# Another stated order for the 2997 steps of a one-core delta-rule and MLP kernel on Trainium2

## The chip, the cores and the metric

The kernel runs on one core of a Trainium2 chip. The metric is the device time of one execution in microseconds (us). A core has five engines that matter here: PE (TensorE, matrix products), DVE (VectorE), ACT (ScalarE), POOL (GpSimd) and SP (SyncE, which here only issues DMAs). Each engine runs its own instructions in order; they wait for each other by semaphores.

## The reference

First a linear attention with a delta rule, step by step over the sequence, for 4 batches x 8 heads, 768 positions, head dimension 48, in fp32; then a layer norm and an MLP with a residual:

```python
k_n = k / (np.linalg.norm(k, axis=-1, keepdims=True) + 1e-06)
for t in range(S):
    y[:, :, t] = einsum('bhd,bhde->bhe', q[:, :, t], state)
    v_old = einsum('bhde,bhd->bhe', state, k_n[:, :, t])
    state = state + beta[:, :, t] * einsum('bhd,bhe->bhde', k_n[:, :, t], v[:, :, t] - v_old)
# x = y with its heads side by side: (4, 768, 384)
xn = (x - mean(x)) / sqrt(var(x) + 1e-06) * g_ln
out = x + maximum(xn @ w_ch1, 0.0) @ w_ch2     # 384 -> 1536 -> 384
```

## The kernel before, in words

The sequence is cut into 12 chunks of 64 positions. Inside a chunk the recurrence becomes matrix products: the products of the keys with themselves (L775), the inverse of a triangular 64 x 64 matrix for each of the 32 heads, the products of queries and keys (L775), and then what goes from chunk to chunk: keys and queries with the state (L983), u (L1017), y (L1024) and the update of the state (L1034).

The inverses are made in three ways. For chunk 0 `first_inverse` works in five levels, for two groups g0 and g1 of 16 heads each: a product E (L722), predicated copies into the matrix on DVE (L731), a product Z (L741), transposes on DVE (L687) and copies back on ACT (L681). For the later chunks `rows_inverse` makes the inverses of 32 x 32 blocks of two chunks in 31 rounds of two DVE instructions (L860, L867); the matrices come in by a DMA (gb) and the inverse goes through DRAM (xd) back to xt. `join` puts two blocks of 32 together: a transposition on DVE (L888) and products e (L898) and z (L904).

After each chunk 256 rows of the MLP are done: layer norm on ACT and DVE (rstd at L967), transposes on PE (L1096) and copies to xnt on ACT (L1088), then the two products with the weights. For the first chunk the first product goes by halves of the columns (L1326, L1341). Later both use fast matrix multiplication: seven products in place of eight for the second (`seven`: products L1423, combinations on POOL L1410, sums on DVE L1441), fifteen in place of sixteen for part of the first (`fifteen`, L1221), and plain products (L1300) for the rest.

No scheduler orders the work when it is built. The functions above only add steps to a list, `Line`; a step is one engine's work (one instruction, or for PE a group of products, most often 16 to 64 small ones or one to four large ones) and it knows which steps it depends on. The text ORDER, at the head of the file, names all 2997 steps in one sequence; `a:b` stands for a run of numbers, and `z` for a filler, two products by the unit matrix whose result is not used (L1515). The steps are emitted in that sequence, and `in_this_order` ties each instruction to the one before it on its own engine and each DMA outside POOL's queue to the one before it in the other queue, so what stands in ORDER is each engine's own order.

```python
def stated_order():
    for t in ORDER.split():
        a, _, b = t.partition(":")
        yield from (-1,) if a == "z" else range(int(a), int(b or a) + 1)
...
for n in stated_order():
    if n < 0:
        self.filler()
        continue
    fn, deps = self.steps[n]
    assert deps <= out and n not in out
    fn()
    out.add(n)
```

Steps named by number in what follows: the inverse of chunk 0 has E and Z of level 1 at 122, 124 and 126, 132 (g0, g1), level 2 at 138, 141 and 144, 150, level 3 at 156, 159 and 162, 168, level 4 at 174, 177 and 180, 186, level 5 at 192, 194 and 196, 200; 175 and 176 are predicated copies of level 4, 193 is the one of level 5 and g0, 187 and 188 are transposes of level 4 and g1. 204 and 205 are the products of queries and keys of chunk 0. 355 and 357 are its u, 359 and 360 its y, 361 to 364 layer norm, 373 to 376 the transposes to xnt, 379 the update of the state. 590 and 588 are the first steps of the first MLP. 337 copies turned keys of chunk 2 on ACT, 389 converts weights there, and 339 and 351 are the products of the keys (L775) of chunks 2 and 3. 327 to 330 read back what the first `rows_inverse` left in xd. 480 to 487 load gb for the second, 556 is the last of its rounds, 557 writes xd and 558 to 565 read it. 625, 699, 704, 961, 967 and 968 are other DMAs that SP issues. 2947 to 2954, 2965 to 2967 belong to the last `seven`: 2953 and 2954 are combinations on POOL.

Of the kernel before, what the change touches and what calls it, by code (L numbers as in the profile page):

```python
# [59 lines left out]
1 9 49 50 8 63 52 51 10 5 250 54 71 11 56 0 6 14 7 12 47 62 53 48 23 13 72 55 36 18 64 42 26 37 61 27 58 60 77 81 15 28 17 32 331 43 73 88 29 40 65 79  # L60
24 19 82 68 78 21 89 74 95 16 76 20 90 75 98 83 80 84 22 85 34 91 86 96 87 33 25 92 97 93 4 35 30 94 110 99 100 111 101 112 114 66 116 122 113 211 210
117 102 70 208 123 115 103 118 233 126 104 124 69 127 105 107 128 119 31 121 106 125 120 252 129 223 132 38 221 138 108 134 39 139 109 222 251 140 135
204 131 130 234 136 3 674 144 137 67 57 133 213 254 146 224 141 149 2 209 413 235 44 142 147 45 253 244 212 143 256 145 150 255 242 205 41 154 153 416
155 243 148 238 151 236 332 152 225 675 156 z 215 157 240 159 158 214 237 239 160 216 162 161 257 46 241 168 164 166 333 206 165 334 245 207 417 163
419 169 174 170 343 258 226 175 172 259 173 415 171 176 381 177 425 260 227 261 167 178 344 217 228 180 179 248 414 263 345 335 386 346 219 182 262
677 186 264 181 420 183 265 266 192 267 268 189 246 336 269 270 218 193 229 220 188 185 184 187 59 271 196 422 190 272 191 231 273 426 194 274 197 199
275 198 421 338 276 247 355 382 277 195 249 384 356 337 359 278 678 279 679 280 200 230 281 361 232 363 387 339 282 364 201 383 391 283 202 203 385
389 373 357 284 375 388 376 374 396 285 590 390 340 358 341 588 591 286 681 342 401 379 287 392 288 289 594 394 290 953 291 347 589 595 292 348 380
293 360 393 350 598 294 362 395 592 368 599 349 442 295 680 441 406 296 351 427 369 815 593 444 297 814 428 443 298 676 602 424 299 352 687 596 300
603 353 301 445 302 399 303 304 377 597 612 305 817 306 606 354 307 418 308 613 607 309 365 423 600 310 397 311 614 689 312 601 366 313 610 314 816  # L70
315 615 611 316 409 604 317 819 318 319 616 818 605 320 404 321 617 322:324 407 608 398 483 325 378 400 402 326 367 629 487 609 370 481 403 371 618
630 480 429 372 446 627 486 485 619 682 628 405 482 633 484 631 329 634 408 330 447 632 410 327 328 448 449 956 479 821 635 820 411 637 809 620 810
638 488 636 621 489:491 641 492 494 622 639 430 493 691 623 495 640 690 496 642 431 497 686 498 624 499 500 822 643 435 434 693 645 501 433 962 502
688 432 503 644 651 957 1100 504 505 436 692 506 507 652 438 508 439 509 647 440 510 437 811 653 511 512 964 450 666 1102 513 654 514 1099 451 515 655
516 517 454 518 965 519 966 1104 520 656 961 455 521 951 456 452 522 463 958 457 646 458 657 453 1215 464 649 465 807 523 459 658 808 524 466 460 1105
525 659 963 467 461 1106 694 950 468 683 462 955 526 660 1112 527 684 1101 528 469 1111 529 473 648 650 695 530 475 474 531 470 476 532 471 661 472
696 533 857 534 1114 535 697 536 967 855 537 858 1213 538 539 685 662 540 856 541 823 542:545 825 546:548 861 663 549:551 863 552 862 553:556 667 867
557 864 968 668 665 869 824 879 868 702 880 959 664 960 859 1214 669 873 860 560 1272 559 672 1103 865 561 812 670 558 705 826 477 866 699 874 698 870
701 888 969 412 706 871 703 885 700 875 704 671 872 1216 566 881 889 625 876 877 895 563 1217 813 567 878 1222 890 564 569 915 882 570 827 562 891 568
886 898 571 565 916 707 1107 896 626 899 572 1115 1212 900 708 883 576 892 709 574 884 901 573 1224 710 1116 893 575 902 954 887 894 917 903 1380 1113  # L80
828 904 1221 1558 711 713 905 829 923 918 577 712 897 924 832 714 715 673 925 716 833 717 906 718 834 926 719 912 835 907 841 836 927 1274 842 919 928
837 1560 908 838 929 920 843 913 839 909 844 941 840 720 910 721 830 845 921 914 846 847 722 922 1377 851 723 578 1264 1223 849 930 724 1557 1226 579
942 725 580 1562 831 931 1218 852 943 850 1118 853 932 848 726 581 1117 933 854 727 582 944 911 728 934 945 729 935 730 970 936 1227 731 938 1376 583
732 937 971 1225 972 585 1273 1228 584 587 1210 1563 733 946 734 1006 952 735 939 736 737 1004 738 974 973 947 1005 739 1007 586 1028 1010 740 1029
1119 1564 1559 975 1229 1011 1031 1008 1561 741 1385 742 1570 940 743 1569 1012 744 1009 745 746 1016 747 1013 976 748 749 1014 1387 750 1017 1572
1386 751 478 1211 979 752 1571 1015 1378 753 754 977 980 755 981 756 1018 1389 757 988 982 989 1384 1573 978 990 1379 1020 983 758:760 1022 761 1021
762 991 984 763 1390 1019 764 1108 985 765 949 1023 1034 1391 766 1230 986 767 948 1109 768 769 1388 1037 770 987 771 1110 1026 772 773 992 774 775
993 994 1038 776 1027 1024 995 1670 1044 1231 996 1030 1120 1265 1025 1275 1047 1035 1121 1039 1064 1040 1048 1122 1045 780 1041 1032 777 1049 1033
778 1065 1042 1036 779 1050 1043 1066 1126 1046 1051 1000 1054 1219 1266 1233 998 1268 997 1232 1276 999 1267 1127 1052 1055 1131 1053 1067 1565 1128
1061 1056 1072 1124 1270 1068 1125 1073 1392 1220 1069 1129 1074 1002 1057 1130 1001 1070 1075 785 1003 784 1058 1269 1076 781 1234 1079 1277 782 1059  # L90
1080 1271 783 1060 1077 1081 1680 2035 1078 786 1373 1062 1090 787 1123 1082 790 1091 789 1083 788 1063 1278 1092 2037 1279 1084 1682 1132 1071 1093
1681 1085 791 1302 1133 1086 1280 793 1134 792 1135 794 1136 1138 795 1094 1284 1137 2039 1139 1140 1235 1141 1285 1142 1281 1143 796 1305 1095 1303
1236 1668 1290 2034 1096 1684 1144 1087 1374 1145 2041 1282 1146 1291 1673 2036 1147 1148 1574 1088 1149 1237 1150 1283 1669 1151 1152 1239 1098 1153
1154 797 1155 1156 1296 1157 799 800 1158 1241 1686 1159 1288 1576 1160 1297 1304 1248 1161 2040 1311 1162 1289 1286 1238 1249 1250 1163 1381 1294
1164 1858 1287 1382 1165 1240 1383 1679 801 1312 1675 1295 1292 1251 1089 1166 1167 1685 1313 1168 1293 1674 1393 1252 1242 1169 798 1253 1855 1308
1243 1395 1375 1309 1244 1857 1306 1245 802 1318 1397 1097 1314 1300 1394 1319 1307 1298 1170 1575 1301 1171 803 805 1172 1246 1321 1173 1315 1247
1174 1322 1299 1255 1316 804 1310 806 1323 1254 1317 1396 1175 1256 1320 1683 1176 2038 1398 1672 1177 1178 1324 1179 1399 1338 1180 1325 1676 1181
1339 1326 1340 1327 1328 1182 1341 1260 1346 1183 1342 1184 1257 1347 1185 1343 1186 1259 1348 1344 1329 1687 1258 1349 1335 1353 1330 1350 1187 1354
1863 1188 1331 1189 1853 1351 1190 1402 1336 1191 1263 1345 1352 1261 1400 1262 1192 1404 1193 1194 1355 1865 1411 1195 1332 1412 1196 1356 1197 1413
1364 1198 1333 1414 1365 1334 1337 1450 1199 1441 1366 1200 1401 1440 1451 1455 1201 1427 1403 2150 1577 1357 1405 1430 1406 1367 1851 1358 1457 1439  # L100
1566 1852 1415 1431 1456 1359 1416 1429 1407 1688 1443 1408 1859 1567 1432 1409 1418 1368 1444 1202 1452 1410 1435 1203 1369 1433 1204 1454 1458 1370
1205 2047 1453 1417 1208 1460 1434 1459 1419 1361 1862 1464 1442 1461 1568 1436 1462 1866 1466 1437 1671 1467 1463 1867 1438 1578 1465 1360 1445 1690
1362 1446 1469 1468 1579 1447 1689 1422 1428 1471 1448 1470 1449 1474 2049 1472 1477 1581 1584 1475 1473 1580 1480 1860 1423 1861 1478 1363 1483 1479
1481 1583 1476 1691 1421 1484 2051 1489 1420 1694 1486 1485 1582 1693 1490 1692 1487 1502 1496 1588 1491 1503 1587 1488 1677 1492 1678 1504 1695 1585
1493 1206 1505 1494 1586 1506 1497 1495 1371 1701 1426 1516 1869 1589 1498 1696 1703 1868 1507 1499 1699 1529 1207 1424 2042 1509 1697 1517 1372 1744
# [1547 lines left out]
```

## Time and profile before

| what | value |
|---|---|
| time, median of three runs | 509.16 us (507.25 to 509.48) |
| span of the profiled execution | 508.8 us, 22190 instructions |
| own time of the profiled execution | not given apart from its span |
| PE busy | 488.6 us (96%), 9606 instructions |
| DVE busy | 353.8 us (70%) |
| POOL busy | 275.6 us (54%) |
| ACT busy | 249.0 us (49%) |
| mean granted clock of PE | 0.965 |
| DMA | 54.99 MB, 108 GB/s over the span |

The span runs from the first instruction to the last of one execution. The profile's page gives the busy time of each engine in 40 slices, the granted clock of PE (`PEclk`, in tenths of full speed), and the chain of work that ended last. In the trace's rows a line reads: start in us, length in us, engine, line, operation, output<-inputs, tile shape, sizes, how many; in brackets the idle time ahead of it and what ended that. Ends of products are modelled and overlap the next start, so differences of starts are used for how long a step takes. "issue" is time for which no wait is seen.

### The profile page before, as it was taken

What the parts mean: (1) busy time and instruction counts of PE and PEld (TensorE: products, weight loads), DVE (VectorE), ACT (ScalarE), POOL (GpSimd) and SP (SyncE); (2) the same over time, 40 slices, a digit from 0 to 9 for tenths busy, and PEclk for the clock granted to TensorE, in tenths of its full rate; (3) what the DMA queues carried; (4) which work ended last, traced back from release to release, by engine and by line L of the source; (5) the groups of instructions that cost most, each with busy time, mean ns of one, the idle gap of its engine ahead of it and who ended that gap; (6) DMA issues with size and microseconds to landing.
All of it is one profiled execution on the core that took longest, in us unless ns stands there. A gap on an engine that the chain in (4) does not pass through costs nothing.

```text
span 508.8 us, 22190 instructions
## 1 busy us (share of the span) xinstructions
PE 488.6 (96%) x9606; PEld 447.6 (88%) x9606; DVE 353.8 (70%) x780; ACT 249.0 (49%) x620; POOL 275.6 (54%) x430
## 2 busy tenths in 40 slices
PE   7778999999899999999999999999999999999996
PEld 3667988788788898899999999999999999999996
DVE  9668987997679648896649898568899328143251
ACT  5758873643544524627435535435563257363230
POOL 5464537264755496438894363492543850645633
PEclk9756799999999999999999999999999999999999
DMA  8988796667656566546834434766154402211101
GB/s 168 293 160 190 249 200 85 98 152 130 90 86 87 187 119 119 65 99 149 194 58 62 94 62 135 150 94 97 50 92 106 111 20 45 60 48 46 24 18 31
DMA packets 196097, 54.99 MB, mean 108 GB/s; under 512 B 186076, under 2 KB 189404, under 8 KB 196000
## 3 DMA queue, kind: packets, MB, share of 16 engines
q1 hardware_dynamic: 189920, 40.58, 41.9%
q10 hardware_dynamic: 3872, 9.83, 6.0%
q0 software_dynamic: 2208, 3.17, 3.8%
q8 instruction: 75, 1.23, 1.0%
q14 instruction: 22, 0.18, 0.1%
HBM read 36.64 MB, written 16.91 MB: 105 GB/s over the span
## 4 chain that ended last, share of the span: by engine, by line
PE 90%; DVE 5%; issue 2%; POOL 1%; DMA 1%; SPq 0%; ACT 0%; DVEq 0%; POOLq 0%; ACTq 0%
PE f L1423 29%; PE f L1221 22%; PE f L1300 9%; PE f L1326 4%; PE f L1341 3%; PE by L983 2%; PE by L1024 2%; PE two L983 2%; PE by L775 2%; PE two L1017 2%; PE two L775 2%; PE two L1034 2%; PE f L775 1%; DMA xt<-xd 1%; PE by L741 1%
## 5 line engine op out<-in xcount | busy, mean ns | idle before, releaser
L1410 POOL TENSOR_TENSOR h_all<-h_all 128x256 f32<-128x256 f32 x123 | 89.9, 742 | 135.1 <-PE f L1423 121.3
L1423 PE MATMUL f<-w_sb,h_all 128*128 128x192 f32 x492 | 109.8, 332 | 1.6 <-DVE rstd L967 1.6
L1423 PEld LDWEIGHTS f<-w_sb,h_all 128*128 128x128 f32 x492 | 81.8, 190 | 3.6 <-issue 1.9
L1423 PE MATMUL f<-words,h_all 128*128 128x192 f32 x396 | 84.5, 330 | 0.3 <-POOL h_all L1410 0.3
L860 DVE TENSOR_TENSOR tmp<-xb,gb 128x87 f32<-128x87 f32 (+21 forms) x186 | 73.7, 396 | 4.9
L867 DVE TENSOR_TENSOR xb<-xb,tmp 128x87 f32<-128x87 f32 (+21 forms) x186 | 73.6, 396 | 4.8
L1241 DVE TENSOR_TENSOR h_all<-h_all,f 128x512 f32<-128x512 f32 x96 | 63.5, 682 | 14.3 <-PE f L1221 13.2
L1423 PEld LDWEIGHTS f<-words,h_all 128*128 128x128 f32 x396 | 66.6, 190 | 1.7 <-POOL h_all L1410 1.0
L1300 PE MATMUL f<-xnt,w_sb 128*128 128x256 f32 x216 | 50.2, 382 | 0.0
L349 POOL DMA_DIRECT2D tb<-in_k_dram x64 | 42.0, 660 | 10.3 <-DVE kt L755 9.4
L1243 ACT ACTIVATE h_all<-h_all 128x512 f32<-128x512 f32 x48 | 28.5, 624 | 34.6 <-DVE h_all L1241 34.3
L1300 PEld LDWEIGHTS f<-xnt,w_sb 128*128 128x128 f32 x216 | 40.2, 190 | 5.3
L1237 ACT COPY h_all<-f 128x512 f32<-128x512 f32 x48 | 26.2, 590 | 34.3 <-PE f L1221 17.4
L1441 DVE TENSOR_TENSOR o<-f,x 128x192 f32<-128x192 f32 x33 | 11.6, 352 | 38.9 <-PE f L1423 22.3
L1221 PE MATMUL f<-words,w_sb 128*128 128x128 f32 x256 | 31.7, 276 | 0.0
L1309 ACT ACTIVATE h_all<-f 128x256 f32<-128x256 f32 x36 | 13.3, 382 | 35.1 <-PE f L1300 34.9
L1221 PEld LDWEIGHTS f<-words,w_sb 128*128 128x128 f32 x256 | 30.0, 192 | 0.2
L1221 PE MATMUL f<-xnt,w_sb 128*128 128x128 f32 x192 | 25.4, 276 | 0.0
L542 POOL TENSOR_TENSOR w_sb<-words 128x768 uint32<-128x768 uint32 (+1 forms) x11 | 15.0, 1365 | 17.7 <-DVE words L529 13.3
L1221 PEld LDWEIGHTS f<-xnt,w_sb 128*128 128x128 f32 x192 | 23.7, 192 | 0.1
L1326 PEld LDWEIGHTS f<-xnt,w_sb 128*128 128x128 f32 x144 | 19.2, 200 | 3.3 <-issue 0.2
L1088 ACT ACTIVATE xnt<-xnt,g_sb 128x256 f32<-128x256 f32 x27 | 12.5, 498 | 19.2 <-DMA xnt<-xld 19.1
(246 smaller groups left out, 958.4 us busy)
## 6 DMA issues: line engine op xcount, KB each, us to landing
words<-in_moe_w_ch_dram ACTq DMA_DIRECT2D x10, 768.0 KB, 5.2
gd<-gsb SPq DMA_DIRECT2D x11, 512.0 KB, 3.6
v<-in_v_dram SPq DMA_DIRECT2D x24, 192.0 KB, 4.3
kr<-in_k_dram SPq DMA_DIRECT2D x46, 96.0 KB, 3.6
out_dram<-o SPq DMA_DIRECT2D x44, 96.0 KB, 2.8
xld<-xlt SPq DMA_DIRECT2D x9, 384.0 KB, 3.3
xnt<-xld SPq DMA_DIRECT2D x36, 96.0 KB, 3.2
gb<-gd SPq DMA_DIRECT2D x44, 64.0 KB, 3.0
```

The lines of the kernel that those rows point to most:

```text
L349: add(eng, cost, lambda: QUEUE[eng].dma_start(out=out_, in_=in_), r, w, bulk=n * ns / 16e3, **kw)
L775: nc.tensor.matmul(pair[hp][half(e ^ (hp & n)), (g * NP + j) * C : (g * NP + j + 1) * C], kt[drows(hp), l], rt[drows(hp), i],)
L860: lambda j=j, n=n, w=w, t=t: nc.vector.tensor_tensor(out=t, in0=xv[:, 0:n, j : j + 1].to_broadcast([np_, n, w]), in1=gv[:, j : j + 1, j + ...
L867: "DVE", dve(n * w), lambda t=t, rest=rest: nc.vector.tensor_tensor(out=rest, in0=rest, in1=t, op=ALU.subtract),
L1221: nc.tensor.matmul(wide(p[:, 128 * n : 128 * n + 128]), w[n // 2][:, n % 2 * 128 : n % 2 * 128 + 128], r, start=start and n == 0, stop=Tru ...
L1237: add("ACT", act(512), lambda: nc.scalar.copy(o, p), pk, ok)
L1241: add("DVE", dve(512), lambda: nc.vector.tensor_tensor(out=o, in0=o, in1=p, op=op), pk, ok)
L1243: add("ACT", act(512), lambda: nc.scalar.activation(o, o, ACTF.Relu), [], ok)
L1300: nc.tensor.matmul(p[:, 0:TOK], w1_sb[:, t, f * 128 : (f + 1) * 128], xnt[:, t], start=(t == 0), stop=(t == KC - 1))
L1326: nc.tensor.matmul(p[:, 0:128], w1_sb[:, t, f * 128 : (f + 1) * 128], xnt[:, t, cols], start=(t == 0), stop=(t == KC - 1))
L1410: add(eng, cost, lambda: e.tensor_tensor(out=out_, in0=x, in1=y, op=op), r, w, port=2 if eng == "Pool" else 1, pr=-2)
L1423: lambda f=f, t=start and f == 0: nc.tensor.matmul(p[:, 0:D2], lhs(f), rhs[:, f], start=t, stop=(f == F2 - 1), skip_group_check=True),
```

## The change

Only the text ORDER is replaced. The 2997 steps, what each does and what each depends on are the same, and so is the filler, which stands in the list once as before. The new list is said to have been found in a model that has semaphores of transfers, turns at PSUM allocations and tile shapes of PE. It uses more runs `a:b`: steps of a kind stand together more often. As the text has fewer lines, a line of code after it has a number lower by 11 (L1423 becomes L1412).

The parts that the prediction speaks of, before (-) and after (+); the rest of the list is reordered in the same manner:

```diff
-204 131 130 234 136 3 674 144 137 67 57 133 213 254 146 224 141 149 2 209 413 235 44 142 147 45 253 244 212 143 256 145 150 255 242 205 41 154 153 416
-155 243 148 238 151 236 332 152 225 675 156 z 215 157 240 159 158 214 237 239 160 216 162 161 257 46 241 168 164 166 333 206 165 334 245 207 417 163
-419 169 174 170 343 258 226 175 172 259 173 415 171 176 381 177 425 260 227 261 167 178 344 217 228 180 179 248 414 263 345 335 386 346 219 182 262
...
-275 198 421 338 276 247 355 382 277 195 249 384 356 337 359 278 678 279 679 280 200 230 281 361 232 363 387 339 282 364 201 383 391 283 202 203 385
-389 373 357 284 375 388 376 374 396 285 590 390 340 358 341 588 591 286 681 342 401 379 287 392 288 289 594 394 290 953 291 347 589 595 292 348 380
...
-2926 2927 2932 2924 2938 2928 2918 2933 2939 2929 2934 2940 2930 2952 2941 2931 2942 2935 2943 2945 2936 2944 2965 2946 2953 2966 2958 2937 2967 2947
-2954 2968 2959 2969 2948 2970 2960 2971 2949 2961 2972 2973 2962 2956 2974 2963 2955 2975 2964 2976 2950 2977 2951 2957 2986 2978 2993 2994 2987 2979
...
+119 120 118 20 21 124 125 132 225 70 235 131 130 128 4 127 136 137 135 105 64 254 256 255 253 41 58 46 37 59 42 38 39 674 57 43 233 67 208 213 210 242
+211 138 29 22 30 139 134 133 3 140 106 107 141 26 142:144 146 145 31 234 226 150 108 236 156 214 109 221 153 155 227 147 149 238 148 223 257 151 243
+157 158 222 152 239 258 28 259 260 162 204 205 163 206 154 244 159 261 164 160 161 263 207 675 224 677 421 332 415 331 417 413 425 423 346 333 334 z
+168 231 166 209 229 240 167 165 237 173 172 171 219 245 212 252 262 241 679 174:176 180 183 381 386 215 169 264 170 265 230 266 181 267:271 177 182
+272 178 179 273 274 192 193 186 275 276 188 216 217 184 248 185 246 190 189 191 277 247 218 196 198 199 197 382 335 187 278:280 383 194 336 343 419
+345 426 420 424 422 355 195 356 228 220 680 676 678 249 384 338 387 200 359 202 201 203 361 391 363 337 385 389 357 281 282 364 283 388 284 285 373
+339 374 375 396 376 358 360 340 362 590 591 368 588 392 390 401 589 286:290 369 291:297 393 298:324 232 250 394 347 379 380 592 594 441 442 593 341
...
+858 950 685 697 557 625 967 704 961 968 861 863 862 867 864 869 372 663 859 870 875 876 868 860 811 823 825 666:671 699 865 866 873 882 883 879 880
+1264 812 561 559 560 558 566 824 672 813 698 881 827 673 871 874 872 888 889 877 890 565 965 701 706 664 700 705 1217 703 702 567 878 898 899 891 826
...
+2940:2943 2931 2945 2946 2944 2932 2933 2952 2965 2958 2934:2937 2953 2966 2947:2949 2954 2950 2967:2970 2959:2961 2971 2973 2951 2974 2975 2962:2964
```

## The prediction

> **What bounds the kernel now.** I began with the engines' shares, the clock and the chain of waits on the profile's page.
>
> ```profile
> PE 488.6 (96%) x9606; PEld 447.6 (88%) x9606; DVE 353.8 (70%) x780; ACT 249.0 (49%) x620; POOL 275.6 (54%) x430
> PE   7778999999899999999999999999999999999996
> DVE  9668987997679648896649898568899328143251
> PEclk9756799999999999999999999999999999999999
> ...
> PE 90%; DVE 5%; issue 2%; POOL 1%; DMA 1%; SPq 0%; ACT 0%; DVEq 0%; POOLq 0%; ACTq 0%
> ```
>
> PE carries 90% of the chain and is full from the fifth slice on (12.7 us each). Only the first 60 us have holes and a clock below full. So an order can change three things: holes early, holes later, and PE's work itself. For the last I read PE's timeline:
>
> ```profile
> 253.19 0.49 PE L1423 MATMUL f<-w_sb,h_all 128*128 128x192 f32 x2
> 253.51 0.49 PE L1423 MATMUL f<-words,h_all 128*128 128x192 f32 x2
> 253.93 1.15 PE L983 MATMUL two<-s_all,kt 48*64 48x48 f32 x64
> 255.01 0.75 PE L904 MATMUL by<-xt,es 32*32 32x32 f32 x64
> 255.69 0.92 PE L1423 MATMUL f<-words,h_all 128*128 128x192 f32 x4
> ```
>
> A product of seven (L1423) starts 0.32 after its like, but 0.42 before a step with small tiles. Over the whole trace it takes 0.325 between its like, 0.418 ahead of and 0.429 behind another tile shape, and a 64-row step of L983 takes 0.968 or, ahead of another shape, 1.078. A visit to small tiles and back thus costs 0.093 + 0.110 + 0.104 = 0.31.
>
> For holes I read the chain in order of time, early, and PE's timeline in the middle and at the end:
>
> ```profile
> 22.97 1.60 issue
> ...
> 28.64 0.85 issue
> ...
> 32.13 1.01 PE by L722 x32
> 33.15 0.91 PE f L741 x32
> 34.05 0.62 PE by L741 x18
> 34.67 1.53 issue
> ...
> 54.46 2.52 PE f L1326 x12
> ```
>
> ```profile
> 137.76 0.49 PE L1423 MATMUL f<-w_sb,h_all 128*128 128x192 f32 x2
> 139.85 0.89 PE L1423 MATMUL f<-w_sb,h_all 128*128 128x192 f32 x4 [1.60 <-DVE rstd L967]
> ...
> 143.84 0.26 PE L898 MATMUL f<-xnj,gsb 32*32 32x32 f32 x8 [0.81 <-issue]
> ...
> 496.00 0.59 PE L1423 MATMUL f<-words,h_all 128*128 128x192 f32 x2 [0.28 <-POOL h_all L1410]
> ```
>
> The "issue" pieces split a step in the middle; early they come every 127 to 128 PE records, wherever those fall (1.10, 1.60, 0.85, 1.53). The hole at 137.76 follows from a DMA: the transposition L888 waits on DVE for xt to return from xd, and the sums and rstd of the MLP stand behind it.
>
> **The sum for before.** Step 590, the first MLP product (L1326), starts at 54.46. The last PE step starts at 504.09. Between them lie 443.14 of PE steps, each at its interval without waits, and so 449.63 - 443.14 = 6.49 of losses. From there to the end are 4.75 (DVE's last sum and the output's DMAs): 54.46 + 443.14 + 6.49 + 4.75 = 508.84, the span. The page has no separate time for the profiled execution; its span is 0.3 below the median 509.16, so I add 0.3 to a span.
>
> **Part 1: tile shapes.** No instruction is added or removed. In the stated lists, the 817 PE steps change tile shape 163 times before and 154 after. All PE intervals without waits sum to 465.71 and 464.49: -1.22. Ahead of step 590 stand 22.57 before and 23.03 after (360 moves ahead of it), so behind it 441.46: **-1.68**.
>
> **Part 2: the prologue.** I walked the new order step by step with before's durations, each engine in its order, each step after its operands.
> (a) Query products 204 and 205 stood inside levels 2 and 3 of the inverse, with their issue pieces 2.36 and 2.02 of the chain. Now both stand behind Z3g0 (162). Of 4.4, the walk gives Z3g0 3.3 (29.6 for 32.9), since ACT's and DVE's copies then come last.
> (b) PE must then do 204, 205, E3g1 (159), the filler and Z3g1 (168) before E4g0 (174); in before 168 alone stood there. Without issue pieces they take 0.76 + 1.17 + 1.01 + 1.15 + 1.16 = 5.25. The record where the 1.53 piece fell is again in 168, the 0.85 one moves into 162. From 29.6 + 0.9 this gives 174 at 35.75 without pieces and 38.1 with both; with faster matmuls if the clock is up, slower copies if not, I take 36.6 to 38.2, middle 37.4 (before 36.58).
> (c) From 174 to the predicated copy 193 of level 5: 7.05, before 7.77, as 175 and 176 follow 174 directly.
> (d) From 193 to 590: 10.1 before. After, the natural transpose 187 stands behind six DVE steps; Z5g1 (200) ahead of y (359); on ACT 337 (0.58) and 389 (0.92) ahead of the copies 374 to 376 that feed 590; on PE 360 ahead of 590, beside 357 and 339 (whose operand came 1.05 late in before). The walk gives 12.35, 1.50 of the excess from the two ACT steps.
> So 590 starts at 37.4 + 7.05 + 12.35 = 56.8: **+2.34**. Bounds: 54.46 if all of (d) is hidden by PE's own work; above, case D.
>
> **Part 3: losses behind 590.** In before: 1.53 on steps 590, 588, 379 and 351; 1.95 at 130.46 and 137.76; 1.01 at 142.34 (0.81 of it issue); 0.72 near 495; 1.28 in crumbs.
> The 1.53 goes, since those operands are ready when 590 comes late. It is part of what +2.34 bought.
> The middle: SP's queue now has seven other issues (625, 967, 704, 961, 968, 699 among them) between the write to xd (557) and its reads (558 to 565). Each costs SP 0.49 to 0.60 (the issues of L349), 7 x 0.55 = 3.9, beside a landing of 3.5 (write at 115.38, reads from 119.21): near zero. The eight loads of gb for this inverse (480 to 487) stand ahead of the reads of the inverse before (327 to 330). So gb lands about 3 earlier, and on DVE 94.97 of work stand ahead of the inverse's end (step 556) for 96.23: it ends near 111.5 for 115.3. The hole wants 1.95: gone. Above, it stays whole if SP's issues are not hidden.
> The end: combinations 2953 and 2954 on POOL (0.74 each) were late for their products. In after 2947 to 2950, 3 x 0.325 more of PE work, stand ahead: -0.72.
> The issue piece stays, 1.0; crumbs 1.28. For new waits I added up, for each result that crosses engines, PE work between its source and its use, less the other queue's work. None is below zero after (two before, both at the end), but 25 places have under 0.4 (4 before). I put 0.4 on all of them together, since before's four cost 0.1 or less where the sum was above zero; bounds 0 and case E.
> Losses after: 1.0 + 1.28 + 0.4 = 2.7: **-3.79**.
> **Sum:** +2.34 - 1.68 - 3.79 = -3.13: span 505.7, **506.0 us**. Its own range: 503.5 to 508.
>
> **The rivals.**
> B, a warm block. The windows have the clock at 0.50 from 30 to 40 us, beside PE busy seven tenths:
> ```profile
> 30.00:40.00 10.00, 7.48 (x213) 6.44 (x211) 5.88 (x21) 4.69 (x14) 4.98 (x6) 0.50 0.82 152
> 50.00:60.00 10.00, 9.97 (x230) 9.02 (x229) 9.69 (x19) 8.20 (x20) 4.61 (x5) 0.68 0.81 260
> ```
> In after, Z3g0 to Z3g1 stand back to back. If full load brings the clock up there as it did at 56.44, 590 comes at 56.0: 505.2. Against it: the issue pieces fall inside the block.
> The Trainium skill, "TensorE: Matmul & The Clock Gate", section "What's actually happening", says that the gate opens after a busy window of about 3.4 us; by that rule the 5.25 us block is long enough for one. The trace agrees in that the clock changes multiples of 3.41 us apart (half from 25.7 to 42.8, full until 46.2, half until 56.44), and shows that PE at seven tenths does not open it.
>
> C, no change. The middle hole stays (1.95), as SP's extra issues delay the reads, and 590 comes at 57.6 (+0.8): 508.8. For it: the SP pieces of 0.49 to 0.60 stand in the chain at 129.43 and 130.08.
>
> D, slower: the lead of (a) does not arise, because Z3g0's operands are bound by the back copies that queue behind weight conversions on ACT. Then 204, 205, 159 and the filler, with their pieces 2.36 + 2.02 + 1.01 + 1.15 = 6.5, come on top of 36.58: 174 at 43, 590 at about 62.7, time 511.9. It decides from 590 past 62.5. For it: ACT holds PE up at 44.50 (0.63, a conversion) and for the copies at 45.05. Against: the DVE steps put first in after are the ones that Z3g0 needs.
>
> E, slower by crumbs: each of the 25 tight places loses what the POOL wait did, 0.25 on average: +6.25, 512.3. It decides from 0.23 each. Against: the crumbs of before, 1.28 in 440 us.
>
> That the change does not do what it says is excluded: in the built instruction lists the shape changes drop and ACT has 17, DVE 12 waits fewer.
>
> **How the numbers follow.** What a measurement can tell here is 0.5%, 2.5 us: faster is below 506.6, slower above 511.7. A (forecast) 0.45: 0.33 faster, as 506.6 lies above its middle and the bounds of (d) reach further down than up, 0.12 same. B 0.10: 0.09 faster, 0.01 same. C 0.13: 0.01, 0.09 and 0.03 slower. D 0.18: 0.02 same, 0.16 slower. E 0.14: 0.01 same, 0.13 slower. Together faster 0.43, same 0.25, slower 0.32. Low end: 590 at 54.46 and crumbs alone, 54.46 + 441.46 + 1.28 + 4.75 + 0.3 = 502.2. High end: D with 1.1 of the middle hole, or E at 0.28 each: 513.0.
>
> **What would show it.** Right: Z3g0 near 29.6, 174 at 36.6 to 38.2, 590 near 56.8, no hole over 1 us at L1423 behind 100 us, no wait on POOL near 495, 444.2 us from 590 to the start of the last PE step. 174 past 41 is D; a hole before L888 is C; many waits of 0.2 to 0.3 behind 60 us are E. The forecast is wrong in kind if PE loses over 4 us behind 590, or 590 starts past 59.

## The result, and the profile after

The changed order takes 524.65 us (median of four runs, 523.28 to 525.76) where the order before takes 509.32 (four runs, 507.25 to 510.09): 1.032 times as long, 95% interval 1.028 to 1.035. It is slower by 15.3 us; 506.0 was forecast and 513.0 was the upper end.

The page of the changed kernel, its first line of busy time, three of the rows of slices and the shares of the chain:

```profile
PE 493.5 (95%) x9606; PEld 450.2 (86%) x9606; DVE 367.0 (70%) x780; ACT 248.9 (48%) x620; POOL 278.6 (53%) x430
...
PE   7577999999999899998999999999999999999996
...
DVE  7598897997699738995748997739998427235151
...
PEclk8665699999999999999999999999999999999999
...
PE 61%; DVE 22%; POOL 5%; issue 5%; DMA 3%; ACT 2%; SPq 0%; DVEq 0%; POOLq 0%; ACTq 0%
```

The same work is done, but DVE is now 22% of the chain where it was 5%, and POOL 5% where it was 1%. DVE's busy time has grown by 13.2 us without one instruction more.

The sum of the prediction, made again on this trace: step 590 starts at 59.80 (54.46 before), the last PE step at 517.10, 441.46 of PE work stand between, so the losses are 15.84 (6.49 before), and 4.79 follow. Against before this is +5.34 for the start, -1.68 for PE's work, +9.35 for the losses and +0.04: +13.05, the difference of the spans (521.88 and 508.84). The medians differ by 2.3 more: a run is 1.7 us longer than its span in each of the later runs, so the profiled run of before, whose own time is not given, would at 508.8 + 1.7 lie above its median, and that of the changed order (523.6) lies below its own. The 0.3 that the prediction added to a span was too little for the same reason.

Where the losses behind 590 lie is seen in windows of 10 us. First before, then after (columns: PE, weight load, DVE, ACT, POOL busy; clock; DMA share; GB/s):

```profile
160.00:170.00 10.00, 10.00 (x266) 8.63 (x268) 9.29 (x25) 7.05 (x22) 2.15 (x4) 1.00 0.75 105
200.00:210.00 10.00, 10.00 (x228) 8.96 (x228) 9.42 (x20) 5.73 (x19) 3.89 (x6) 1.00 0.65 103
```

```profile
160.00:170.00 10.00, 10.00 (x167) 8.71 (x166) 9.69 (x12) 4.70 (x15) 9.47 (x15) 1.00 0.31 56
200.00:210.00 10.00, 9.03 (x290) 7.57 (x279) 9.45 (x23) 4.74 (x13) 7.52 (x13) 1.00 0.73 126
```

From 160 to 170 us POOL is busy 9.47 of 10 where it was busy 2.15, and from 200 to 210 it is busy 7.52 for 3.89. DVE is as busy as before, but from 160 to 170 it gets through 12 instructions in place of 25. The two windows do not hold the same instructions; like for like, the twelve instructions of the rounds of 252 down to 207 elements take 9.2 us (162.49 to 171.72) where they took 5.1 (160.16 to 166.14, less the 0.87 of a state update in between). The timelines of DVE and POOL in the changed kernel show why:

```profile
162.49 2.78 DVE L849 TENSOR_TENSOR tmp<-xb,gb 128x252 f32<-128x252 f32 x1
165.30 0.69 DVE L856 TENSOR_TENSOR xb<-xb,tmp 128x252 f32<-128x252 f32 x1
166.03 1.11 DVE L849 TENSOR_TENSOR tmp<-xb,gb 128x247 f32<-128x247 f32 x1
167.17 0.42 DVE L856 TENSOR_TENSOR xb<-xb,tmp 128x247 f32<-128x247 f32 x1
```

```profile
162.49 0.74 POOL L1156 TENSOR_TENSOR pt<-w_sb,pt 128x256 f32<-128x256 f32 x1
163.17 0.73 POOL L1156 TENSOR_TENSOR q_last<-w_sb 128x256 f32<-128x256 f32 x1
163.85 0.72 POOL L1156 TENSOR_TENSOR pt<-qt,w_sb 128x256 f32<-128x256 f32 x1
164.53 0.45 POOL L1438 TENSOR_TENSOR words<-h_all 128x128 f32<-128x128 f32 x1
164.93 1.30 POOL L338 DMA_DIRECT2D tb<-in_k_dram  x2
```

A round's instruction that takes 0.42 alone lasts 2.78 beside four POOL instructions in a row, and ends 0.3 after the last of them, when POOL has turned to issuing DMAs. What it delays is the update of the state, step 978 (L1033): its operand was ready at 166.38, it started at 172.02 behind eleven rounds' instructions, and PE waited:

```profile
173.02 1.16 PE L764 MATMUL two<-kt 48*64 48x64 f32 x64 [1.62 <-DVE s_all L1033]
```

I call "stretch" what the rounds' instructions last beyond nearly the shortest of the same size in the two traces (the very shortest would add 3.4 to each figure below and change no difference). It is 25.7 us before and 37.3 after; for the third and fourth inverse, 130 to 240 us, 3.6 and 4.6 before and 7.4 and 9.3 after. The collision itself is not new: of the 310 rounds' instructions behind the first inverse, 62 had a two-operand POOL instruction beside them for over 60% of their time before, and 67 after. What has moved is where it falls: during the rounds of the third and fourth inverse such POOL work overlaps them for 12.1 us before and 19.3 after.

### The profile page after: what moved, and what is told of

It reads as the page before. It is cut to its first block, busy times and chain, and to the rows that moved or that the text cites. A ratio compares the mean times of both kernels' runs of the same rounds, so it can differ in the third digit from the quotient of the medians.

```text
span 521.9 us, 22159 instructions
## 1 busy us (share of the span) xinstructions
PE 493.5 (95%) x9606; PEld 450.2 (86%) x9606; DVE 367.0 (70%) x780; ACT 248.9 (48%) x620; POOL 278.6 (53%) x430
## 4 chain that ended last, share of the span: by engine, by line
PE 61%; DVE 22%; POOL 5%; issue 5%; DMA 3%; ACT 2%; SPq 0%; DVEq 0%; POOLq 0%; ACTq 0%
PE f L1210 19%; PE f L1412 19%; DVE xb L856 7%; DVE tmp L849 7%; PE f L1315 3%; PE f L1330 2%; POOL h_all L1399 2%; PE f L1289 2%; PE by L1013 2%; PE by L972 1%; PE two L972 1%; PE two L1006 1%; DMA words<-in_moe_w_ch_dram 1%; PE by L764 1%; PE f L557 1%
## 5 line engine op out<-in xcount | busy, mean ns | idle before, releaser
L1399 POOL TENSOR_TENSOR h_all<-h_all 128x256 f32<-128x256 f32 x123 | 91.9, 761 | 115.2 <-PE f L1412 93.8
L1412 PE MATMUL f<-w_sb,h_all 128*128 128x192 f32 x492 | 97.1, 330 | 1.5 <-POOL h_all L1399 0.7
L849 DVE TENSOR_TENSOR tmp<-xb,gb 128x87 f32<-128x87 f32 (+21 forms) x186 | 80.0, 430 | 6.5 <-POOL xb L836 1.9
L1412 PEld LDWEIGHTS f<-w_sb,h_all 128*128 128x128 f32 x492 | 80.5, 190 | 3.2 <-POOL h_all L1399 1.2
L856 DVE TENSOR_TENSOR xb<-xb,tmp 128x87 f32<-128x87 f32 (+21 forms) x186 | 78.8, 424 | 4.9
L1412 PE MATMUL f<-words,h_all 128*128 128x192 f32 x396 | 77.6, 331 | 0.4 <-POOL h_all L1399 0.2
L1412 PEld LDWEIGHTS f<-words,h_all 128*128 128x128 f32 x396 | 64.9, 190 | 3.2 <-POOL h_all L1399 1.3
L1232 ACT ACTIVATE h_all<-h_all 128x512 f32<-128x512 f32 x48 | 28.5, 623 | 44.5 <-DVE h_all L1230 44.3
L1289 PEld LDWEIGHTS f<-xnt,w_sb 128*128 128x128 f32 x216 | 40.0, 190 | 6.8 <-DVE o L1339 1.2
L1430 DVE TENSOR_TENSOR o<-f,x 128x192 f32<-128x192 f32 x33 | 11.4, 351 | 45.4 <-PE f L1412 36.4
L1210 PE MATMUL f<-words,w_sb 128*128 128x128 f32 x256 | 33.2, 277 | 0.8 <-POOL words L1186 0.8
L531 POOL TENSOR_TENSOR w_sb<-words 128x768 uint32<-128x768 uint32 (+1 forms) x11 | 15.8, 1441 | 33.7 <-DVE words L518 23.1
L1210 PEld LDWEIGHTS f<-words,w_sb 128*128 128x128 f32 x256 | 30.7, 192 | 1.2 <-POOL words L1186 0.9
L1298 ACT ACTIVATE h_all<-f 128x256 f32<-128x256 f32 x36 | 13.1, 381 | 27.6 <-PE f L1289 27.4
L1210 PEld LDWEIGHTS f<-xnt,w_sb 128*128 128x128 f32 x192 | 23.5, 192 | 0.6 <-ACT xnt L1077 0.3
L1186 POOL TENSOR_TENSOR words<-xnt 128x128 f32<-128x128 f32 x32 | 14.6, 469 | 17.2 <-ACT xnt L1077 17.1
L1051 ACT ACTIVATE x<-by 128x384 f32<-128x384 f32 x23 | 11.1, 484 | 25.7 <-PE by L1013 17.6
```

Of the source, the lines that this page charges most:

```text
L531: lambda: nc.gpsimd.tensor_tensor(out=dst.bitcast(U32), in0=shape(hi), in1=shape(lo), op=ALU.add),
L849: lambda j=j, n=n, w=w, t=t: nc.vector.tensor_tensor(out=t, in0=xv[:, 0:n, j : j + 1].to_broadcast([np_, n, w]), in1=gv[:, j : j + 1, j + ...
L856: "DVE", dve(n * w), lambda t=t, rest=rest: nc.vector.tensor_tensor(out=rest, in0=rest, in1=t, op=ALU.subtract),
L1210: nc.tensor.matmul(wide(p[:, 128 * n : 128 * n + 128]), w[n // 2][:, n % 2 * 128 : n % 2 * 128 + 128], r, start=start and n == 0, stop=Tru ...
L1232: add("ACT", act(512), lambda: nc.scalar.activation(o, o, ACTF.Relu), [], ok)
L1289: nc.tensor.matmul(p[:, 0:TOK], w1_sb[:, t, f * 128 : (f + 1) * 128], xnt[:, t], start=(t == 0), stop=(t == KC - 1))
```

## The experiments

The table gives, for each run, the median time, the ratio with its interval, and from its trace the start of step 590, the losses behind it (here the sum over steps, up to 0.3 less than above) and the stretch. The ratio is to runs of the kernel before that were taken beside each run; their medians lie between 507.80 and 509.32, so it is not the time over 509.32. The last three columns stand on one execution each, and 590 varies by some 3 us between executions with the same start (51.4 to 54.5 in before, e1 and e10, 59.8 to 62.7 in the changed kernel, e2 and e6). s1, s2 and s4 have two executions each; those of s4 are 5.0 apart.

| kernel | time | ratio | 590 | losses | stretch |
|---|---|---|---|---|---|
| before | 509.32 | | 54.5 | 6.2 | 25.7 |
| changed | 524.65 | 1.032 (1.028 to 1.035) | 59.8 | 15.6 | 37.3 |
| e1_start_before | 519.61 | 1.023 (1.019 to 1.026) | 51.4 | 16.3 | 35.5 |
| e2_start_after | 515.81 | 1.014 (1.009 to 1.019) | 62.7 | 5.4 | 28.5 |
| e3_memset_after | 518.76 | 1.020 (1.017 to 1.024) | 60.9 | 9.6 | 23.6 |
| e3_memset_before | 506.25 | 0.995 (0.993 to 0.997) | 53.3 | 3.7 | 16.6 |
| e5_no_reads_after | 514.55 | 1.012 (1.009 to 1.016) | 59.4 | 5.5 | 3.9 |
| e5_no_reads_before | 505.20 | 0.994 (0.991 to 0.996) | 52.6 | 2.4 | 4.2 |
| e6_urgent | 525.29 | 1.033 (1.030 to 1.036) | 60.3 | 16.4 | 35.4 |
| e7_loads | 525.11 | 1.035 (1.031 to 1.038) | 59.1 | 16.3 | 37.3 |
| e8_holes | 524.97 | 1.032 (1.027 to 1.036) | 60.2 | 15.8 | 37.6 |
| e9_holes_lost | 510.22 | 1.003 (1.000 to 1.006) | 54.5 | 6.1 | 25.5 |
| e10_best | 507.22 | 0.996 (0.994 to 0.997) | 53.9 | 3.6 | 25.8 |
| e11_chain | 527.12 | 1.036 (1.033 to 1.040) | 63.2 | 16.2 | 38.9 |
| s1_before_to_174 | 524.03 | 1.030 (1.026 to 1.034) | 58.3 | 17.3 | 36.4 |
| s2_before_to_194 | 522.93 | 1.028 (1.023 to 1.033) | 57.4 | 16.5 | 35.9 |
| s3_after_to_174 | 511.41 | 1.006 (1.002 to 1.009) | 56.1 | 6.4 | 27.1 |
| s4_after_to_194 | 514.73 | 1.012 (1.000 to 1.024) | 58.7 | 3.7 | 26.9 |

**One cause or two.** As the steps are the same, two orders can be joined: a first part of the one, then what is left, in the order of the other.

```diff
 ORDER of e1_start_before
-<the changed order>
+<the order before, up to and with 590>
+<the changed order without these steps>
```

> The steps up to and with 590 stand as before, all others in the changed order. Theory 1 (two separate places: 590 starts 5.3 us later in the changed kernel, and 9.3 us more of waits arise behind it by themselves): the 5.3 come back and the rest stays, 519.3 us, the waits behind 590 stay at about 15 us. Rival 2 (the late start alone puts the engines behind it out of step): the waits shrink with it, about 509 us.

> The reverse: the steps up to and with 590 in the changed order, all others as before. Theory 1: 590 starts near 59.8, the waits behind it are like those of before (6 us): 514.6 us or less, as some of the 5.3 are waits that only moved. Rival 2: waits arise behind it although its order is the old one, 520 us or more.

519.61 and 515.81: two places, and they add up to about the whole (10.3 and 6.5 over 509.3, together 16.8 for 15.3; over 508.44, the runs beside them, 18.5). 515.81 is 1.2 more than theory 1 allowed, as 590 came at 62.7 in place of 59.8. With the old start the losses behind 590 stay at 16.3; with the old rest they are 5.4, although 590 comes at 62.7. Theory 1 holds.

**The rounds beside POOL.** First (e3) only the combinations for the fast products were made to read nothing; then (e5) all of POOL's two-operand instructions, as here for one of them:

```diff
-add(eng, cost, lambda: e.tensor_tensor(out=out_, in0=x, in1=y, op=op), r, w, ...)
+add(eng, cost, lambda: idle(e, out_) if eng == "Pool" else e.tensor_tensor(...), r, w, pr=-2)
...
+def idle(e, out):
+    for _ in range(2):
+        e.memset(out, 0.25)
```

> The changed order; POOL's combinations for the fast products (L1399 and L1186) are replaced by two memsets each of the same tile, so they read nothing from SBUF and the output is not the reference's. Theory 1a (the rounds of the inverses on DVE, two SBUF operands each, stretch when POOL works beside them, 29.5 us over their shortest in the trace for 19.8 before, and PE waits for what is queued behind them): the stretch falls below 12 us, the waits behind 590 by 6 to 9 us, 516 to 519 us. Rival 3 (the order itself: too many rounds stand ahead of a step that PE needs): the stretch may fall, the waits stay above 12 us, 522 us or more.

> The same replacement in the order of before. Theory 1a: the stretch of the rounds falls by a like share, but few waits hung on it: 507 to 509 us, so the distance between the two orders falls from 15 to 8 to 11 us. Rival 3: 507 to 509 us as well, and the distance stays at 14 to 15 us.

> The changed order; every two-operand instruction of POOL (L531, L611, L1156, L1186, L1399, L1430, L1438) is replaced by two memsets of its output, so POOL reads almost nothing and the output is not the reference's. Theory 1a (stretched rounds on DVE eat the room that the new order leaves): the stretch falls from 37 us in all to under 8, the losses behind 590 from 15.6 to 4 to 6, 510 to 514 us. Rival 3 (the order by itself queues too much ahead of urgent steps): the stretch falls, the losses stay above 8, 516 us or more.

> The same replacement in the order of before. Both theories: 503 to 506 us with losses of 3 to 4 behind 590. By theory 1a the distance between the two orders falls from 15 to 7 to 8, nearly all of it the late start; by rival 3 it stays at 12 or more.

(The first text counts the stretch without the first inverse.) The half measure takes away 13.7 of the stretch and 6.0 of the losses, more stretch being left than expected, since the third and fourth inverse collide mostly with other POOL work (6.0 and 6.2 left). The full one takes the stretch away, 3.9, and the losses fall to 5.5; the distance between the orders' losses shrinks from 9.4 to 3.1. So about two thirds of it goes with POOL's reads, and 3.1 stay without any stretch. The times agree with theory 1a more than with rival 3, though less cleanly than forecast: the two orders are 15.3 apart as they are, 12.5 with the half measure (8 to 11 was expected, 14 to 15 by the rival) and 9.4 with the full one (7 to 8, or 12 or more). The groups of rounds by line, changed order and e5_no_reads_after (busy us, mean ns; the lines are 3 lower down there):

```profile
L849 DVE TENSOR_TENSOR tmp<-xb,gb 128x87 f32<-128x87 f32 (+21 forms) x186 | 80.0, 430 | 6.5 <-POOL xb L836 1.9
```

```profile
L852 DVE TENSOR_TENSOR tmp<-xb,gb 128x87 f32<-128x87 f32 (+21 forms) x186 | 62.7, 337 | 5.5 <-POOL xb L839 0.9
```

POOL is not idle in that run (241.5 us busy for 278.6). 81 rounds' instructions behind the first inverse have a memset beside them for over 60% of their time, and last 0.01 longer than the shortest; in the changed kernel 67 have a two-operand POOL instruction beside them, and last 0.34 longer, 0.66 for 0.33. So the rounds are stretched by what POOL reads, not because it works. The caveat: the memsets are also shorter and wait for fewer operands, which takes away the PE waits that POOL itself causes (some 2 of the 15.6). No run has POOL reading as long as before but away from the rounds, so how much of the fall in losses is the rounds' alone is not shown to the last us.

The Trainium skill, "SBUF — State Buffer", section "Who interferes with whom", states this rule: a DVE instruction with two SBUF inputs contends with a GpSimd instruction that reads SBUF and not with one that only writes, and the one that is issued later blocks. The trace agrees on what contends (0.34 and 0.01). On who blocks it does not, by the starts on record: a DVE instruction is held through four POOL instructions in a row (2.78 for 0.42), and one of 0.4 is held for 2.73 though it is on record as started 0.96 ahead of the POOL instruction that it outlasts. From the changed order, DVE and POOL:

```profile
221.60 2.73 DVE L856 TENSOR_TENSOR xb<-xb,tmp 128x240 f32<-128x240 f32 x1
```

```profile
222.56 1.49 POOL L611 TENSOR_TENSOR v<-v,knrm 128x768 f32<-128x768 f32 x1
```

**Queue or stretch.** Were the rounds simply in the way?

```diff
-... 750:760 978 ...       (likewise 453, 929, 1234, 796, 1327, 1755)
+... 978 750:760 ...
```

> The changed order, but seven steps on DVE (453, 929, 978, 1234, 796, 1327, 1755) are moved ahead of the 4 to 18 steps, mostly rounds of an inverse, that stood between the moment their operands were ready and their start. Theory 1b (the waits are for these queued rounds, whether stretched or not): the waits at 103, 145, 170, 201, 207, 234 and 287 go, some 6.5 us, 517 to 519.5 us. Rival 4 (DVE has too much work, the wait only moves to the next step or to the end of the inverse): under 2 us gained, 522.5 us or more.

525.29: nothing gained. The waits are on other steps now, as the two views of PE's waits behind 62 us show, changed order and e6_urgent (us in total, times, longest):

```profile
PE two L764 <- DVE s_all L1033: 2.1, 2, 1.6
PE f L1210 <- DVE h_all L1230: 0.9, 1, 0.9
PE f L1412 <- POOL h_all L1399: 0.9, 3, 0.6
```

```profile
PE by L1013 <- issue: 2.2, 2, 2.0
PE f L1412 <- POOL h_all L1399: 1.7, 4, 0.7
PE f L1289 <- DVE o L1339: 1.1, 1, 1.1
```

The wait for the state is gone, others have come. Theory 1b falls and rival 4 holds: in these stages DVE has little time left (busy 9.69 and 9.45 of 10 us in the two windows above), so what is moved ahead delays what it passes. (1.2 of the new losses is a longer issue piece at L1013, which the edit did not aim at.)

**The late start.** Three edits, each undoing one thing, and one in the order before:

```diff
 e7_loads:  416 344 57 59 674 from the first lines to behind 141
 e8_holes:  z behind 156, 335 behind 180, 336 behind 192
 e11_chain: first_inverse's steps on DVE and ACT ahead of what they stood behind when ready
 e9_holes_lost (order before): 335 behind 196, 336 behind 194, z behind 159
```

> The changed order, but the five early loads that it had put ahead of the others (416, 344, 57, 59 on SP and POOL, and 674, the blocks of k) stand behind step 141 again. Theory 5 (the piece of 3.7 us without a wait in step 126 is the instruction stream held up by these transfers): the piece falls to 1.0 to 1.4, step 124 starts near 17.3, and 590 comes 1 to 2.6 earlier, 522 to 523.5 us. Rival 6 (the piece does not hang on these transfers): it stays above 3, no change at 524.6 us.

> The changed order, but three PE steps stand again where they stood before, in the waits of the inverse: the filler behind 156, the turned keys 335 behind 180 and 336 behind 192. Theory 7 (the 5 us that 193 to 590 takes longer are PE work that the new order took out of waits and put on the path, at half clock 1.0 to 1.1 each): 590 comes 2.0 to 3.0 earlier, near 57.3, 521.5 to 522.5 us. Rival 8 (the copies on ACT and DVE set 590, PE's work there is hidden): 590 stays within 0.7 of 59.8 and the time at 524 us or more.

> The reverse: the order of before, with 335 moved behind 196, 336 behind 194 and the filler behind 159, as in the changed order. Theory 7: 590 comes 2 to 3 later than the 51.4 to 54.5 of the runs with the old start, 510.5 to 511.5 us. Rival 8: no change, 508 to 509.5 us.

> The changed order, but in the start the steps of the first inverse on DVE and ACT (copies, transposes, copies back, and u 358) stand ahead of the conversions of weights and of the steps of the next inverse that stood between the moment they were ready and their start (0.6 to 5.5 us each). Theory 9 (the late start is this queueing: the chain of the first inverse waits on DVE and ACT): 168 comes near 36, 194 near 45.5, 590 at 55 to 57 for 59.1 to 62.6, 520 to 521.5 us. Rival 10 (the delayed conversions and rounds are themselves wanted at 590, or the clock and the pieces without a wait set it): 590 stays past 58.5, 523.5 us or more.

None brings the start back. In e7 the issue piece in step 126 goes, from start to start, from 3.96 only to 2.56. Z3g0 then starts at 29.09, but later waits eat the gain (PE's wait ahead of the filler is 2.4 for 1.7, two for ACT's copies grow to 0.9 and 1.0), and 590 comes at 59.1. In e8 PE's work moves into waits (335 starts at 41.7 for 47.7), but 194 still starts at 49.2 (48.9) and 590 at 60.2, so PE's work was hidden and rival 8 holds there; e9 takes 510.2, between the two forecasts, with 590 at the upper end of the runs with the old start. e11 is slower still, 1.036, with 590 at 63.2 for the 55 to 57 of theory 9; rival 10 holds. One round there waited for two conversions of POOL, lines of DVE and of POOL in e11_chain:

```profile
55.15 3.64 DVE L856 TENSOR_TENSOR xb<-xb,tmp 64x207 f32<-64x207 f32 x1
```

```profile
55.66 2.89 POOL L531 TENSOR_TENSOR w_sb<-words 128x768 uint32<-128x768 uint32 x2
```

With 590 still unexplained, the start was cut at two points, from both sides:

> The steps up to and with 174 as before, all others in the changed order. Theory 11 (the start loses at two places: 3.8 up to 174, where the two query products, a product of level 3 and the filler stand in one block, and 3 to 5 behind 193, where u, y and the copies stand in another): 174 at 32.5 to 36.6, 590 at 54.5 to 58. Rival 12 (one early cause, the loads and the held up instructions, carries through): 590 at 51.4 to 54.5 as with the whole old start.

> The same up to and with 194. Theory 11: 194 at 42.8 to 45.6, and 11 to 12 from there to 590 as in the changed kernel, where before needs 8.6 to 9.0: 590 at 54 to 57. Rival 12: 590 at 51.4 to 54.5.

> The changed order up to and with 174, all others as before. Theory 11: 174 at 37 to 39.5, then 18 to 19 to 590 as before: 590 at 55.5 to 58, time 511 to 513 us. Rival 12: 590 at 59 or more, as with the whole new start.

> The changed order up to and with 194, all others as before. Theory 11: 194 at 47.5 to 50.6, then 8.6 to 9.0: 590 at 56.5 to 59.5, time 512 to 514 us. Rival 12: 590 at 59 or more.

| part of the start, us | old order | new order | s1 | s2 | s3 | s4 |
|---|---|---|---|---|---|---|
| 162 to 174 | 1.3 to 3.6 | 7.0 to 8.0 | 2.3 | 1.7 | 7.5 | 7.4 |
| 174 to 193 | 7.3 to 8.6 | 6.1 to 7.0 | 9.4 | 8.2 | 7.0 | 6.4 |
| 193 to 194 | 1.7 to 1.9 | 3.2 to 4.5 | 2.8 | 1.7 | 1.7 | 3.1 |
| 194 to 590 | 8.6 to 9.1 | 10.9 to 12.1 | 10.9 | 13.6 | 8.3 | 10.5 |

(Every step by its start, 193 too. Old: before, e1, e3_memset_before, e5_no_reads_before, e10. New: changed, e2, e3_memset_after, e5_no_reads_after, e6, e7, e8.) Mostly, each part costs what its own order costs, whatever stood before it; the clear exceptions are 174 to 193 in s1, which should cost 6.1 to 7.0 and took 9.4, and the last part in s2 and s4. So theory 11 holds in kind: the block from Z3g0 to E4g0 costs about 5, 174 to 193 gives 1.5 back, and what follows 193 costs 4 to 5. Its numbers were a little small: s1 and s2 end 0.3 to 0.4 past the upper bound, the last part took 13.6 in s2 and 10.5 in s4 for 11 to 12 and 8.6 to 9.0, and the time of s4, 514.73, is 0.7 past its own. Rival 12 is out in s1 to s3 and, with 58.7 for 59, only just in s4. Inside the block, PE's timeline of the changed order shows what was priced and what was not:

```profile
31.17 1.09 PE L730 MATMUL f<-xt,xt 64*64 64x64 f32 x29 [1.98 <-ACT words L513]
...
33.83 1.03 PE L711 MATMUL by<-qt,gsb 64*64 64x32 f32 x30
36.55 1.22 PE L1504 MATMUL f<-ident 128*128 128x256 f32 x2 [1.69 <-DVE qt L676]
37.70 1.14 PE L730 MATMUL by<-xt,xt 64*64 64x64 f32 x32
```

Product 159 is done at 34.87, but its copies on DVE (160, 161) run at 36.43 to 36.88, behind a step that prepares the next inverse (260, 1.68 long), two transposes and the masks of the queries. The 1.68 is the same collision: 260 ran from 33.43 to 35.11 beside a conversion of weights on POOL (33.57 to 35.05), and it lasts 0.18 in e5_no_reads_after. There 174 starts at 37.84 for 38.61, but 590 still comes at 59.4 (52.6 with the old order and no reads), behind ACT copies that wait for a conversion of weights, so the collision does not explain the late start. Which of DVE, ACT and the half clock sets each of the two parts stays open.

**What is good in it.** From the two traces an order can be made that beats both: the order before, with the one hole of 1.76 closed and the changed order's last part.

```diff
-... 577 714 715 673 716 717 718 719 929 ...   (on DVE)
+... 714:719 577 929 673 ...
-<from 2926 on: the order before>
+<from 2926 on: the changed order>
```

> The order of before with two edits: on DVE the first six rounds 714 to 719 go ahead of 577, which waits for a transfer, and 673 behind the sum 929; from step 2926 on the changed order's last part is used. The wait of 1.76 at 137.8 and the 0.7 near 495 go: 2 to 2.5 us less than before, 505.5 to 507 us. Rival: the first only moves the wait to the end of that inverse, 0.7 us less or no change that can be told.

507.22, 0.996 of before (0.994 to 0.997): 1.9 less than the 509.09 of the runs beside it, just short of the 2 to 2.5 expected. It is faster by a margin that is clear but small. PE does not wait at the two places, 137.8 and near 495, where the holes were, and the largest wait left behind 62 us is 0.4, at 140.13; its timeline in e10_best:

```profile
136.56 0.49 PE L1422 MATMUL f<-w_sb,h_all 128*128 128x192 f32 x2
136.88 0.49 PE L1422 MATMUL f<-words,h_all 128*128 128x192 f32 x2
137.21 1.14 PE L1422 MATMUL f<-w_sb,h_all 128*128 128x192 f32 x6
138.28 0.94 PE L1033 MATMUL two<-u,kr 64*48 64x48 f32 x64
```

## Why the prediction was wrong

**Part 1, tile shapes: right to some tenths.** With the forecast's -1.68 the four terms give the measured span, but that is no test, as the losses are what is left over. The test is the losses added up step by step: 15.6 for the 15.84 left over, and 6.2 for 6.49 before. So -1.68 fits to a few tenths. That is no measurement of the 0.31 by itself.

**Part 2, the start: later, as forecast, but by more than twice as much.** +2.34 was forecast, +5.34 came, and at 59.8 step 590 is past the 59 that the prediction itself had named as a sign of being wrong in kind. (a) Z3g0 got a lead of 1.8 (31.17 for 32.94), not 3.3: the issue piece in step 126 was 3.74 for 1.10, and PE waited 1.98 ahead of Z3g0 for a copy on ACT that stands behind a conversion of weights. (b) From there to 174 it was 7.4; the walk had 7.8, but that was luck: the two issue pieces that it put there did not come, and in their place PE waited 1.69 for the DVE steps named above, with the clock at half from 31.6 on. The walk used durations of a trace in which DVE was busy 5.88 of 10 from 30 to 40 us; in the changed order it is busy 9.41. So 174 came at 38.6 for 37.4. (c) 174 to the end of 193 took 7.05, as forecast. (d) From there to 590 it was 14.1, not 12.35. Why stays open: from 40 to 60 us DVE is no busier than before, and without any stretch, in e5_no_reads_after, (d) takes 15.0. The bound "54.46 if all of (d) is hidden" was too kind: in no run with the whole changed start is 590 ahead of 59.

**Part 3, the losses: wrong, and this is the step that failed.** -3.79 was forecast, +9.35 came, 13.1 of the 16.2 us between the forecast span and the measured one. The holes that it called gone are gone or smaller (no wait for the transfer at the transposition, L888, behind the hole at 137.76; 0.79 ahead of step 941 for 1.76; 0.3 near the end for 0.7). For the one in the middle this was luck: the rounds of that inverse did not end near 111.5 but at 117.9, after the 115.3 of before, and the last read from xd was issued at 134.94 for 131.15. The wait is gone because the transposition itself comes later, at 141.33 for 135.79. But the 25 tight places got 0.4 together, as each result's room was counted with the durations of before's trace. Those durations hold only where POOL reads beside a round as much as it did there. The new order puts more of POOL's work beside the rounds of the third and fourth inverse (19.3 us for 12.1), these rounds take longer, and the room is used up: eight DVE steps kept PE waiting for 0.3 to 1.7, 6.7 in all. Six of them (929, 978, 1234, 796, 1327, 1755) cost 5.2, and the rounds that they queued behind were stretched by 9.1 in that time. In the order before 978, 1234, 1327 and 1755 started within 0.2 of the moment they were ready. Of the 9.4 more losses 6.3 go when POOL reads nothing; the cause of the other 3.1 stays open.

**Rivals.** E, many crumbs, was nearest in kind, with 0.25 at 25 places; it came as 12 places of 0.3 to 1.7, 9.7 in all. D was partly right about the start, as the copy on ACT in (a) does queue behind a conversion, but it gave 62.7, since it had no lead at all, and it had no price for the rest. C was wrong, that wait at L888 went. B was wrong the other way: the clock stayed at half until 62.4, beside PE busy 6.8 to 9.2 of each 10 us from 30 to 60. None of the rivals had the two engines' collision, which stands in the page of the Trainium skill named above and in before's own trace, in rounds of 0.60 for 0.32 beside POOL.

## What to carry to other kernels

A count of work against work, made with durations of one order, holds for another order only if the same engines work side by side; before using it, split the durations of an engine by what its neighbour does at the time. Room of 0.2 to 0.4 us is room only for durations that don't vary more than that. Where two orders of the same steps are at hand, joining the head of one to the tail of the other locates a loss in two runs, better than undoing suspects one by one.

## What the runs showed of the hardware

DVE instructions with two operands in SBUF lasted up to 3.3 us longer beside POOL instructions that read SBUF (3.64 for 0.35 in e11_chain, 2.78 for 0.42 in the changed order; mean 0.34 longer where over 60% overlaps), through several of POOL's in a row, and also where the DVE instruction is on record as started first (221.60 for 222.56). POOL's hardly lengthened: those of 128x256 have a median of 0.75 with a round beside them and 0.73 without. Beside memsets on POOL the rounds lasted 0.01 longer. PE's issue pieces early in the kernel vary much more than one trace shows: from start to start, the one in step 126 was 0.3 to 1.4 with the old start and 2.2 to 4.0 with the changed one, the one in 204 1.8 to 4.3 with the old start. And PE's clock stayed at half for 30.7 us (31.6 to 62.4) in the changed kernel while PE was busy 7.8 to 9.2 of each 10 us from 40 to 60.
